# A gated attention and bilinear-FFN mix on one core: gate sums in the K/V projection, Q moved inside SBUF, and the front written as one list of operations

## The chip, the core and the metric

The kernel runs on one core of a Trainium2 chip. Five engines work side by side: TensorE (PE, with the loads of its stationary operand shown as PEld), VectorE (DVE), ScalarE (ACT), GpSimd (POOL), and SyncE (SP), whose queue here issues nearly all transfers. Each engine takes its own instructions strictly in the order in which the kernel wrote them, and waits where one of them needs something that another engine or a transfer has not yet delivered. The metric is the device time of the program in microseconds (us), lower is better. Before the change it is 1620.87 us, the median of three runs (1620.53 to 1621.84).

## The reference

The input `x` is 2048 tokens of 512 numbers. Attention has 32 heads of size 16 that share one K and one V; the other branch is a bilinear FFN with 1792 inner columns; a sigmoid gate per token mixes both.

```python
x = A_x
g = _sigmoid((x * gate_w).sum(-1, keepdims=True))
# a: attention
q = (x @ wq).reshape(B, S, H, Dh).transpose(0, 2, 1, 3)    # H = 32, Dh = 16
k = x @ wk
v = x @ wv
p = _softmax(jnp.einsum("bhqd,bkd->bhqk", q, k) * (Dh ** -0.5), axis=-1)
a = jnp.einsum("bhqk,bkd->bhqd", p, v).transpose(0, 2, 1, 3).reshape(B, S, H * Dh) @ wo
# b: bilinear FFN
b = jnp.einsum("bsf,fd->bsd", (x @ w_gate) * (x @ w_up), w_down)
return g * a + (1 - g) * b
```

All is fp32. The kernel writes a product of two fp32 matrices as three products of a rounded high part and a low remainder (hi·hi, lo·hi, hi·lo), which `mm3` lists.

## The kernel before, in words

**Units.** The attention is cut into 64 units, one for each chunk `c` of 512 tokens, group `g` of 8 heads (128 columns of `wq`) and tile `t` of 128 tokens. For each unit PE computes the scores twice. The first pass (S1, the function `p1`) puts queries on partitions and keys along the row, 512 keys at a time; DVE takes the maximum of each 512 keys (`mx`). Sixteen steps (4 head slots by 4 key chunks `kq`), each with two halves, give 32 maxima for a unit. `p1_end` folds them into one maximum per query and head, DVE splits it into two parts, four small DMAs store it in DRAM (`dm`), and two DMAs fetch it as two extra rows of the unit's `Q` tile. The second pass (S2, `p2`) then computes the scores with keys on partitions and the maximum already taken off, ACT takes the exponential into a `P` tile, and `pv` multiplies `P` with V (`acc`). `osb`, `do`, `raw`, `rb` and `oT` belong to the division and transposition of the result. Two halves of 64 array rows run side by side on PE, called lanes here, and S1, S2 and all the products of the steady part go out on lane 0 or lane 1.

**Filler.** The projections of Q for the other chunks and groups, the FFN and the product with `wo` are cut into jobs of 12 products per lane (`Job`), which are woven between S1, S2 and `pv`. In the first chunk, group 0's Q is projected in the front, and groups 1 to 3 are jobs.

**What sets the order.** The front (from `x_trans0` to the last `kv`) is written out by hand. Then a planner takes over: the class `State` counts with fixed costs and due times, and a loop first gives the lead: S1 until both lanes have `LEAD` = 25 steps, and `LEADJOBS` = 6 jobs of filler. After the lead, tokens of the string `ORDER` say which of S1, filler, S2 or `pv` comes next; the first S2 of unit 0 is held back in the plan until `mat[0]`, the time at which its maximum should have come back. On the chip PE waits there for the fetch itself. `later` and `at` place work of the other engines and queues by the plan's clock.

**The front.** The chunks of `x` are loaded in order (`load_x`), transposed by PE into `px` banks (`x_trans0`, `x_trans`), copied by ACT to a high part and subtracted by DVE or POOL to a low part (`split`). `kv` multiplies with `wkvt`, a 128-column weight that holds K three times (high, low, high rows for the three products of S1) and V, for 512 tokens at once; ACT and DVE write `KK`, ACT a copy for V, which `v_trans` transposes. Q of group 0 is stored to DRAM and fetched by `q_fetch` with six DMAs for each unit, since a unit's `Q` tile has another arrangement of partitions. In the trace below, L296 is the DVE step that finishes `KK`, L700 the maximum, L143 a DVE split, L303 the copy of V.

**Gate.** The sum of `x * gate_w` per token is taken in the lead: POOL multiplies (L320), ACT sums with an accumulator (L324), 16 times; `gates` then makes the sigmoid.

Of the kernel before, what the change touches and what calls it, by code (L numbers as in the profile page):

```python
# [21 lines left out]
D = 512  # L22
# [26 lines left out]
LEADJOBS = 6  # L49
# [6 lines left out]
)  # L56

# [11 lines left out]
def mix_kernel(ctx: ExitStack, tc: tile.TileContext, x, wq, wk, wv, wo, wg, wu, wd, gw, out):  # L69
# [34 lines left out]
    z = consts.tile([128, NC * NT], F32, name="z")  # L104
# [58 lines left out]
    def load_x(c):  # L163
        if c < 2:
            xn = [w512("y", F32, 8) for _ in range(NT)]
        else:
            pairs = [work.tile([128, 2, 512], F32, name="P", tag="P", bufs=PBUF) for _ in range(2)]
            xn = [t[:, i] for t in pairs for i in range(2)]
        for t in range(NT):
            eng = nc.scalar if c == 0 and t == NT - 1 else nc.sync  # L170
            eng.dma_start(xn[t], x2[c * 512 + t * 128:c * 512 + t * 128 + 128, :])
        return xn
# [33 lines left out]
    def q_store(c, g, qh, ql):  # L206
        dq[c, g] = []
        for src in (qh, ql):
            d = dram.tile([128, 512], F32, name="dq", tag="dq", bufs=2 * NC * NG)
            nc.sync.dma_start(d, src.bitcast(F32))  # L210
            dq[c, g].append(d)
        dqat[c, g] = clock["T"] + 4500.0
# [5 lines left out]
    def q_fetch(u):  # L218
        c, g, t = units[u]
        q = Q[u] = work.tile([128, 4, 128], F32R, name="Q", tag="Q", bufs=QB)  # L220
        for d, rows in zip(dq[c, g], ((0, 32), (16,))):
            for half in range(2):
                for r in rows:
                    b = half * 64 + r
                    src = d[half * 64:half * 64 + 64, t * 128:(t + 1) * 128]
                    nc.sync.dma_start(q[b:b + 16].bitcast(F32), src.rearrange("(s d) q -> d s q", d=DH))
        qat[u] = clock["T"] + 6000.0

    kvn = work.tile([128, 4, 32], F32, name="kvn", tag="oT", bufs=2)
    nc.scalar.dma_start(kvn[:, :, 0:16], wk_v)  # L230
    nc.scalar.dma_start(kvn[:, :, 16:32], wv_v)
    xns = {0: load_x(0)}
    wqn = [stage(wq_v[:, :, 0:128])]
    xns[1] = load_x(1)
    xns[2] = load_x(2)
    xns[3] = load_x(3)
    wqs = [[w512("wh", F32R, WB), w512("wl", F32R, WB)] for g in range(NG)]
    kvs2 = [work.tile([128, 4, 32], F32R, name=n, tag=n, bufs=2) for n in ("rb", "raw")]
# [4 lines left out]
    def kv_split():  # L243
# [8 lines left out]
        split2(*wqs[0], wqn[0])  # L252

    def x_trans0():
        xT[0] = x_tiles()
        hi, lo = xT[0][2:]
        for t in range(NT):
            p = bank(2 + t, "px")
            for k in range(4):
                nc.tensor.transpose(p[:, KS[k]], xns[0][t][:, KS[k]], ident)  # L260
            split(hi[:, :, KS[t]], lo[:, :, KS[t]], p.rearrange("p (k q) -> p k q", k=4))
            if t == 1:
                kv_split()

    def x_trans(c, ks=range(4), pool=()):
        xn = xns[c]
        if c not in xT:
            xT[c] = [[w[:, k] for k in range(4)] for w in (woh, wol)] if c == 3 else \
                x_tiles((("hh", "hl"), ("wdh", "wdl"))[c - 1])
        for k in ks:  # L270
            p = bank(2 + (4 * c + k) % 5, "px")
            for t in range(NT):
                nc.tensor.transpose(p[:, KS[t]], xn[t][:, KS[k]], ident)  # L273
            if k in pool:
                xs = w512(("yt", "osb")[k % 2], F32, 2)
                nc.scalar.copy(xT[c][0][k], p)
                nc.scalar.copy(xs, p)
                nc.gpsimd.tensor_tensor(xT[c][1][k], xs, xT[c][0][k].bitcast(F32), op=OP.subtract)
            else:
                split(xT[c][0][k], xT[c][1][k], p)  # L280

    kvs = {}

    def kv(c, between=None):
        p = ms_bank(c % 2)
# [3 lines left out]
        mm_all(p, prods[:6], True, False)  # L289
        if between:  # L290
            between()
        mm_all(p, prods[6:], False, True)
        Kc = KK[:, c * 512:(c + 1) * 512]
        kvs[c] = w512("gs", F32, 3)
        nc.scalar.activation(Kc, p, AF.Identity, bias=kneg)
        nc.vector.scalar_tensor_tensor(Kc, Kc.bitcast(F32), klow, p, op0=OP.mult, op1=OP.add)  # L296
        nc.scalar.copy(kvs[c], p)

    def v_trans(c):
        pv = bank(7, "pv")  # L300
        for t in range(4):
            nc.tensor.transpose(pv[:, t * 128:(t + 1) * 128], kvs[c][:, t * 128:(t + 1) * 128], ident)  # L302
        nc.vector.tensor_copy(V[:, c * 4:(c + 1) * 4, 0:DH].rearrange("p t (h d) -> p t h d", h=2),  # L303
                              pv.rearrange("p (t h c) -> p t h c", t=4, h=2)[:, :, :, 50:58])
# [8 lines left out]
    gate_left = [(c, t) for c in (2, 3, 0, 1) for t in range(NT)]  # L313

    def gate_sum():
        if not gate_left:
            return
        c, t = gate_left.pop(0)
        scr = w512("yt", F32, 2)
        nc.gpsimd.tensor_tensor(scr, xns[c][t], gwb, op=OP.mult)  # L320
        end = spend("pool", 1240.0)

        def add():
            nc.scalar.activation(scr, scr, AF.Copy, accum_out=z[:, c * NT + t:c * NT + t + 1])  # L324
            spend("act", 700.0)
            gate_sum()
# [674 lines left out]
```

## Time and profile before

| | us |
|---|---|
| median of 3 runs | 1620.87 |
| the profiled execution's own time | 1621.27 |
| its span in the profile | 1619.5 |
| PE busy in the span | 1610.8 (99%) |
| DVE busy | 1381.0 (85%) |
| ACT busy | 1245.7 (77%) |
| POOL busy | 744.7 (46%) |
| first S1 on PE | 22.44 |
| last row of the front on PE, first row of the lead | 31.87, 32.19 |
| 32 maxima of unit 0 done, fold begins on DVE | 49.41 |
| first S2 on PE | 58.74 |
| first `acc` product on PE | 70.08 |

A page of the profile describes one execution. A timeline row gives the start, the length, the engine, the line and operation, the tiles, how many of them run on in one stretch (x15), and in brackets the idle time ahead and what ended it. A chain row gives a start, a length and the work that the end of the program hangs on. A matmul's modelled length is longer than the distance to the next one, so the pace of PE is read from starts, or from a count over a stretch. Rows of SPq are the issue of a DMA, not its transfer.

### The profile page before, as it was taken

The page shows a single profiled execution, that of the slowest core. Times are in us where ns is not written, and L with a number is a line of the kernel's source. Part 1 is how long each engine was busy: PE and PEld are TensorE (multiplying, and loading weights), DVE is VectorE, ACT ScalarE, POOL GpSimd, SP SyncE. Part 2 cuts the span into 40 slices and gives each one's busy share as a digit, 9 for nine tenths or more (in the row PEclk, how much of TensorE's full clock was granted, in tenths as well). Part 3 has the DMA queues.
Part 4 walks back from the last instruction along what each step waited for, and adds up shares of the span by engine and source line. Part 5 has one row for each costly group of instructions (what it writes and reads, how often), then busy time and mean ns, then how long its engine had stood idle before and what let it go on. Part 6 is the DMA issues. An engine that isn't in the chain of part 4 may idle for free.

```text
span 1619.5 us, 35319 instructions
## 1 busy us (share of the span) xinstructions
PE 1610.8 (99%) x13126; PEld 1042.4 (64%) x13126; DVE 1381.0 (85%) x2410; ACT 1245.7 (77%) x2411; POOL 744.7 (46%) x876
## 2 busy tenths in 40 slices
PE   9999999999999999999999999999999999999998
PEld 7666666666666666666666666576566666666664
DVE  6988888888898888888888888888888898898870
ACT  4787777777788787787778787787788787787785
POOL 5515652624644642635443651643743641642732
PEclk9999999999999999999999999999999999999999
DMA  4463322212312221212231221222231221222101
GB/s 161 174 212 114 97 67 59 61 54 72 102 58 72 66 73 54 65 52 69 64 100 62 71 66 57 64 59 65 62 111 52 68 79 53 62 65 60 36 25 38
DMA packets 184991, 121.44 MB, mean 75 GB/s; under 512 B 46196, under 2 KB 154356, under 8 KB 184820
## 3 DMA queue, kind: packets, MB, share of 16 engines
q1 hardware_dynamic: 183620, 118.87, 24.5%
q8 instruction: 103, 1.69, 0.4%
q14 instruction: 68, 0.56, 0.1%
q10 hardware_dynamic: 1200, 0.33, 0.1%
HBM read 82.96 MB, written 36.17 MB: 74 GB/s over the span
## 4 chain that ended last, share of the span: by engine, by line
PE 97%; DVE 1%; ACT 1%; issue 0%; POOL 0%; POOLq 0%; ACTq 0%
PE ms L872 34%; PE acc L753 29%; PE s L740 18%; PE s L699 15%; DVE mx L700 1%; PE ms L150 1%; ACT P L741 1%; PE px L273 0%; PE wo L150 0%; PE warm L764 0%; ACT yt L361 0%; PE pv L302 0%; PE pick L672 0%; PE px L260 0%; DVE rb L675 0%
## 5 line engine op out<-in xcount | busy, mean ns | idle before, releaser
L700 DVE TENSOR_REDUCE mx<-s 128x1 f32<-128x512 f32 x2048 | 1306.9, 684 | 171.2 <-PE s L699 87.9
L741 ACT ACTIVATE P<-s 128x512 f32<-128x512 f32 x2048 | 1077.9, 605 | 257.1 <-PE s L740 188.0
L740 PE MATMUL s<-Q,KK 50*128 50x512 f32 x2048 | 750.3, 411 | 0.1
L699 PE MATMUL s<-KK,Q 48*128 48x512 f32 x2048 | 692.7, 407 | 0.1
L753 PE MATMUL acc<-P,V 128*32 128x512 f32 x4096 | 492.9, 598 | 0.0
L740 PEld LDWEIGHTS s<-Q,KK 50*128 50x128 f32 x2048 | 352.6, 185 | 175.6 <-issue 97.2
L699 PEld LDWEIGHTS s<-KK,Q 48*128 48x128 f32 x2048 | 338.6, 185 | 104.0 <-ACT P L741 47.3
L872 PE MATMUL ms<-xh,wh 64*128 64x512 f32 x920 | 338.9, 391 | 0.0
L872 PE MATMUL ms<-xl,wh 64*128 64x512 f32 x920 | 336.5, 391 | 0.0
L872 PE MATMUL ms<-xh,wl 64*128 64x512 f32 x920 | 322.6, 392 | 0.0
L753 PEld LDWEIGHTS acc<-P,V 128*32 128x32 f32 x4096 | 107.9, 109 | 236.2 <-issue 195.4
L535 POOL TENSOR_TENSOR hf<-gs 128x512 f32<-128x512 f32 x56 | 72.0, 1285 | 351.8 <-ACT gs L526 337.0
L362 POOL TENSOR_TENSOR y<-y,yt 128x512 f32<-128x512 f32 x79 | 101.5, 1288 | 233.4 <-ACT yt L361 229.8
L872 PEld LDWEIGHTS ms<-xl,wh 64*128 64x128 f32 x920 | 164.6, 186 | 8.2
L872 PEld LDWEIGHTS ms<-xh,wh 64*128 64x128 f32 x920 | 163.5, 185 | 9.6 <-issue 0.4
L872 PE MATMUL ms<-wdh,hh 64*128 64x512 f32 x448 | 164.6, 393 | 0.0
L872 PE MATMUL ms<-wdl,hh 64*128 64x512 f32 x448 | 164.2, 391 | 0.0
L872 PEld LDWEIGHTS ms<-xh,wl 64*128 64x128 f32 x920 | 157.8, 186 | 9.8 <-issue 0.3
L872 PE MATMUL ms<-wdh,hl 64*128 64x512 f32 x448 | 158.9, 392 | 0.0
L138 POOL TENSOR_TENSOR wl<-wn,wh 128x512 fp32r<-128x512 f32 x116 | 149.5, 1289 | 9.3
L757 ACT COPY osb<-acc 128x512 f32<-128x512 f32 x64 | 37.6, 587 | 75.8 <-PE acc L753 75.8
L635 POOL TENSOR_TENSOR oT<-raw,rb 128x128 f32<-128x128 f32 x63 | 29.1, 463 | 128.3 <-DMA rb<-dr 128.3
(149 smaller groups left out, 1343.4 us busy)
## 6 DMA issues: line engine op xcount, KB each, us to landing
do<-osb SPq DMA_DIRECT2D x63, 256.0 KB
wn<-in_B_w_gate_dram SPq DMA_DIRECT2D x56, 256.0 KB
wn<-in_B_w_up_dram SPq DMA_DIRECT2D x56, 256.0 KB
wdn<-in_B_w_down_dram SPq DMA_DIRECT2D x56, 256.0 KB
Q<-dq SPq DMA_DIRECT2D x384, 32.0 KB
raw<-do SPq DMA_DIRECT2D x252, 32.0 KB
dq<-oh SPq DMA_DIRECT2D x16, 256.0 KB
dq<-ol SPq DMA_DIRECT2D x16, 256.0 KB
```

The lines of the kernel that those rows point to most:

```text
L138: nc.gpsimd.tensor_tensor(lo, src, hi.bitcast(F32), op=OP.subtract)
L150: nc.tensor.matmul(p, l, r, start=start and i == 0, stop=stop and i == len(prods) - 1)
L362: nc.gpsimd.tensor_tensor(y[c, t], y[c, t], tmp, op=OP.add)
L535: nc.gpsimd.tensor_tensor(hf, gu[0], gu[1], op=OP.mult)
L635: nc.gpsimd.tensor_tensor(dst, raw[:, 0], rb, op=OP.mult)
L699: nc.tensor.matmul(p, q[r, slot], KK[r, kq * 512:(kq + 1) * 512], start=True, stop=True)
L700: nc.vector.tensor_reduce(mx[u][:, half * 4 + slot, kq:kq + 1], p, axis=AX.X, op=OP.max)
L740: nc.tensor.matmul(p, KK[r, j * 128:(j + 1) * 128], q[r].rearrange("p s q -> p (s q)"), start=True, stop=True)
L741: nc.scalar.activation(P[s][:, half], p, AF.Exp, scale=0.25)
L753: nc.tensor.matmul(acc[u][b:b + 32, :], V[:, j + i], src[:, half], start=(j == 0), stop=(j == NJ - 2))
L757: nc.scalar.copy(osb, acc.pop(u))
L872: nc.tensor.matmul(p, lhs[HALVES[l]], rhs[HALVES[l]], start=(i == 0 and (l == 0 or j.apart)), stop=(end and (l == 1 or j.apart)))
```

## The change

It has four parts.

1. **Gate sums.** `gate_w` is loaded as 4 rows of 128 (`gwn`), transposed by PE, and becomes a 33rd column of the K/V weight (`kvn`), split with it and placed in column 58 of `wkvt`. The projection `kv` then yields the gate's sum as one of its 128 rows; `v_evac` takes its exponential with ACT, 4 columns for a chunk. The 16 products of POOL, the 16 sums of ACT, the load of `gwb` and the tile `z` are gone.
2. **Q from SBUF to SBUF.** Q of chunk 0, group 0 is projected in two halves of 256 tokens (`q_first` 0 and 4). Units 0 and 1 need the first half; `q_move` carries it from the split tile to `Q` with six DMAs for each unit, no DRAM between. For the other units `q_store` now writes six pieces (high, low, high, two halves each) with six DMAs for a job instead of two, arranged so that `q_fetch` needs two DMAs for a unit instead of six. The columns of `wq` are permuted when split (`wq_split`), which gives this arrangement.
3. **The front as one list.** The string `FRONT` names each operation of the front by a letter and numbers: D, C and L load, T transposes, X and P split (P with POOL), K is a quarter of a `kv` product, E its evacuation, V and U the transposition of V and its evacuation, J a quarter of a Q product, Z its evacuation, M a move, N, A and W weight splits, S one half of an S1 step. Q of group 1 joins the front, so `FRONTQ` = (2, 3) are left as jobs, and `LEADJOBS` is 5.
4. **Order of S1.** `order1` begins with key chunk 0 of unit 0 and of unit 1, then goes on with chunks 1 to 3 of unit 0. Unit 0 has its 32 maxima after 40 half steps instead of 32. The front holds 22 half steps instead of 8; the lead still ends at 25 steps a lane.

Rows of the built program show three places. First PE, from the end of chunk 1's `kv` product to the first S1 rows. `px` are transposes of x, `s` is S1, `pv` the transposition of V. Before:

```order
L150 MATMUL ms_325<-hl,P 128x512
L302 MATMUL pv<-ident,gs 128x128 x4
L273 MATMUL px<-ident,P 128x128 x8
L699 MATMUL s_367<-KK,Q 128x512
L699 MATMUL s_370<-KK,Q 128x512
```

and after, from the transposition of chunk 0's V on:

```order
L318 MATMUL pv<-ident,gs 128x128 x4
L281 MATMUL px<-ident,P 128x128 x4
L157 MATMUL kv<-hh,P 128x512 x2
L157 MATMUL kv<-hl,P 128x512
L157 MATMUL kv<-hh,P 128x512 x2
L157 MATMUL kv<-hl,P 128x512
L729 MATMUL s_335<-KK,Q 128x512
L729 MATMUL s_342<-KK,Q 128x512
L729 MATMUL s_345<-KK,Q 128x512
```

S1 began behind the whole product of chunk 1 (its last row is the first one shown) and 8 transposes of chunk 3. Now its first three halves stand inside chunk 1's product (`kv<-hh`), ahead of all transposes of chunk 3, and the groups of S1 that follow alternate with the rest of the front.

Second SP, from the store of unit 0's maximum (`dm<-mt`) to its fetch (`Q<-dm`) and the next fetch of a unit (`Q<-dq`). `dq` is the store of a Q job. Before:

```order
L720 DMA dm<-mt 8x2x32 x4
L226 DMA Q<-dq 16x4x128 x6
L210 DMA dq<-oh 128x512
L210 DMA dq<-ol 128x512
L727 DMA Q<-dm 2x512 x2
L226 DMA Q<-dq 16x4x128 x6
```

and after:

```order
L750 DMA dm<-mt 8x2x32 x4
L222 DMA dq<-oh 64x512 x2
L222 DMA dq<-ol 64x512 x2
L222 DMA dq<-oh 64x512 x2
L757 DMA Q<-dm 2x512 x2
L234 DMA Q<-dq 48x4x128 x2
```

Eight issues stood between the store and its fetch. Now six stand there, all of one job (chunk 0, group 3); the first of them waits for ACT and the third for POOL to deliver that job.

Third POOL, in the stretch from the end of the front into the lead. Before, the products of the gate (L320) stand among the low parts of Q (L344):

```order
L320 TENSOR_TENSOR yt<-P,osb 128x512 x8
L320 TENSOR_TENSOR yt<-y,osb 128x512
L344 TENSOR_TENSOR ol<-gs,oh 128x512
L320 TENSOR_TENSOR yt<-y,osb 128x512 x2
L344 TENSOR_TENSOR ol<-gs,oh 128x512
L320 TENSOR_TENSOR yt<-y,osb 128x512 x2
L344 TENSOR_TENSOR ol<-gs,oh 128x512
L320 TENSOR_TENSOR yt<-y,osb 128x512 x3
L344 TENSOR_TENSOR ol<-gs,oh 128x512 x7
```

and after they are gone; splits of x (L294, `wdl` and `wol`) stand where POOL now ends the front, then the last split of `wq` (L144, L145) and the low parts of Q (L370):

```order
L294 TENSOR_TENSOR wdl<-yt,wdh 128x512
L294 TENSOR_TENSOR wol<-yt,woh 128x512
L294 TENSOR_TENSOR wol<-osb,woh 128x512
L144 CAST wh<-wn 128x512
L145 TENSOR_TENSOR wl<-wn,wh 128x512
L370 TENSOR_TENSOR ol<-gs,oh 128x512
L370 TENSOR_TENSOR ol<-gs,oh 128x256
L370 TENSOR_TENSOR ol<-gs,oh 128x512 x9
```

POOL has 16 instructions of 512 columns less in the lead, and three splits of x more in the front.

From the first S2 on, PE's rows are the same in both programs, row for row but for line numbers, and so are ACT's but for the gate's exponential (L330), which is no longer there. Ahead of it PE has 50 halves of S1, 64 transposes of x and the same number of products in both, except that 12 products of 512 columns are now 24 of 256, and one transpose of 4 columns is added.

The diff, cut to its core:

```diff
-LEADJOBS = 6
+LEADJOBS = 5
+FRONT = """
+D1 D3 T01 X01 D0 L0 D2 T03 T00 T02 A0 C1 X00 X03 J00 J01 N X02 J02 J03 T10 C2 L1 T12 K00 K01 Z0 T11 M0 X12 K02 K03 P10
...
+FRONTQ = (2, 3)
...
     def q_store(c, g, qh, ql):
-        dq[c, g] = []
-        for src in (qh, ql):
-            d = dram.tile([128, 512], F32, name="dq", tag="dq", bufs=2 * NC * NG)
-            nc.sync.dma_start(d, src.bitcast(F32))
-            dq[c, g].append(d)
+        d = dq[c, g] = dram.tile([2, 3, 64, 512], F32, name="dq", tag="dq", bufs=NC * NG)
+        for r, src in enumerate((qh, ql, qh)):
+            for half in range(2):
+                nc.sync.dma_start(d[half, r], src[HALVES[half]].bitcast(F32))
...
-        for d, rows in zip(dq[c, g], ((0, 32), (16,))):
-            for half in range(2):
-                for r in rows:
-                    b = half * 64 + r
-                    src = d[half * 64:half * 64 + 64, t * 128:(t + 1) * 128]
-                    nc.sync.dma_start(q[b:b + 16].bitcast(F32), src.rearrange("(s d) q -> d s q", d=DH))
+        for half in range(2):
+            src = dq[c, g][half, :, :, t * 128:(t + 1) * 128]
+            nc.sync.dma_start(q[half * 64:half * 64 + 48].bitcast(F32), src.rearrange("r (d s) q -> (r d) s q", s=4))
...
+    gwn = work.tile([128, 128], F32, name="gwn", tag="rb", bufs=2)
+    nc.scalar.dma_start(gwn[0:4], gw.rearrange("(k p) -> k p", p=128))
...
+            eng.tensor_copy(w[:, :, 0, 58:59], kvs2[v][:, :, 32:33])
+    def wq_split(g, fn):
+        n = wqn[g].rearrange("p (m s d) -> p m d s", s=4, d=DH)
+        fn(*[w.rearrange("p (m d s) -> p m d s", d=DH, s=4) for w in wqs[g]], n)
...
+    def v_evac(c):
+        pv = vp.pop(c).rearrange("p (t h c) -> p t h c", t=4, h=2)
+        nc.vector.tensor_copy(V[:, c * 4:(c + 1) * 4, 0:DH].rearrange("p t (h d) -> p t h d", h=2), pv[:, :, :, 50:58])
+        nc.scalar.activation(gb[:, c * NT:(c + 1) * NT], pv[:, :, 0, 58], AF.Exp, scale=-1.0)
...
-        nc.gpsimd.tensor_tensor(scr, xns[c][t], gwb, op=OP.mult)
...
-            nc.scalar.activation(scr, scr, AF.Copy, accum_out=z[:, c * NT + t:c * NT + t + 1])
...
+    def q_first(g, i):
+        if i == 0:
+            qp[g] = hold(("q", g), "q")
+        cols = slice(0, 256) if g == 0 else slice(256, 512) if g == NG else slice(0, 512)
+        prods = [(w, xk[:, cols]) for w, xk in proj(wqs[g % NG], xT[0])]
+        mm_all(qp[g][:, cols], prods[3 * i:3 * i + 3], i == 0, i == 3)
+    def q_move(u):
+        qh, ql = qp["s"]
+        Q[u] = work.tile([128, 4, 128], F32R, name="Q", tag="Q", bufs=QB)
+        for r, src in ((0, qh), (32, qh), (16, ql)):
+            for half in range(2):
+                b = half * 64 + r
+                eng = nc.scalar if u == 0 and half else nc.sync
+                eng.dma_start(Q[u][b:b + 16].bitcast(F32), src[HALVES[half], KS[u]].bitcast(F32))
...
-    order1 = [(0, slot, kq) for kq in range(4) for slot in range(4)]
-    order1 += [(u, slot, kq) for u in range(1, NU) for slot in range(4) for kq in range(4)]
+    order1 = [(u, slot, 0) for u in range(2) for slot in range(4)]
+    order1 += [(u, slot, kq) for u in range(2) for kq in range(1, 4) for slot in range(4)]
+    order1 += [(u, slot, kq) for u in range(2, NU) for slot in range(4) for kq in range(4)]
...
+    nc.tensor.transpose(p[:, 0:4], gwn[0:4], ident[0:4, 0:4])
+    nc.vector.tensor_copy(kvn[:, :, 32], p[:, 0:4])
...
+    for op in FRONT.split():
+        acts[op[0]](*map(int, op[1:]))
```

More of the change, by code (lines that the diff above doesn't have):

```diff
@@ L251, in kv_split @@
             eng.tensor_copy(w[:, :, :, 50:58], kvs2[v][:, :, 16:32].rearrange("p k (h d) -> p k h d", h=2))
[L252 to L263, printed above, removed]
@@ L265, in x_trans @@
-    def x_trans(c, ks=range(4), pool=()):
-        xn = xns[c]
-        if c not in xT:
[L268 to L280, printed above, removed]
@@ L561, in ffn_jobs @@
         for c in range(NC):
-            yield from q_jobs(c, range(c == 0, NG))
+            yield from q_jobs(c, FRONTQ if c == 0 else range(NG))
         pend = None
```

164 lines of the change are left out of this document (84 added, 80 removed).

## The prediction

> **What bounds the kernel now.** I read the page's engines first, then the chain of waits over the first 75 us, since all that moves stands there, then the timelines of DVE, SP and PE.
>
> ```profile
> PE 1610.8 (99%) x13126; PEld 1042.4 (64%) x13126; DVE 1381.0 (85%) x2410; ACT 1245.7 (77%) x2411; POOL 744.7 (46%) x876
> ```
> ```profile
> 8.82 5.73 PE ms L150 x24
> 14.56 3.86 PE px L273 x32
> ...
> 40.32 9.07 DVE mx L700 x15
> 49.41 0.20 DVE mm L708
> ...
> 50.33 9.57 DVE mx L700 x16
> 59.94 0.50 PE s L699
> ```
>
> PE bounds the whole, but up to 59.94 the chain hangs on DVE's maxima: PE has no free bank until DVE has read one. From 59.94 on the chain is PE's alone. PE's rows are the same in both programs from the first S2 on, so what the change is worth is the shift of that point, and the question is when PE can run S2 at full pace.
>
> ```profile
> 57.90 0.97 PE L699 MATMUL s<-KK,Q 48*128 48x512 f32 x3
> 58.74 0.49 PE L740 MATMUL s<-Q,KK 50*128 50x512 f32 x1
> ```
> ```profile
> 58.74:63.74 5.00, 4.81 (x34) 3.18 (x35) 5.00 (x9) 3.98 (x8) 1.28 (x1) 1.00 0.77 272
> 63.74:68.74 5.00, 5.00 (x43) 3.60 (x41) 4.45 (x8) 4.84 (x10) 1.29 (x1) 1.00 0.17 62
> ```
>
> First S2 starts at 58.74. The second fence counts instructions in stretches of 5 us (PE's in the first bracket): 34, then 43. The 9 that are missing are 9/43 of 5 us, 1.05 us that DVE's backlog costs behind the first S2.
>
> **The change, part by part.** First when S1 can start. Its rate and start before, and the prices of PE's pieces:
>
> ```profile
> 22.98 1.29 DVE L700 TENSOR_REDUCE mx<-s 128x1 f32<-128x512 f32 x2
> ```
> ```profile
> 5.50 0.59 ACT L142 CAST xh<-px 128x512 fp32r<-128x512 f32 x1 [1.88 <-PE px L260]
> 6.12 1.51 DVE L143 TENSOR_TENSOR xl<-px,xh 128x512 fp32r<-128x512 f32 x2 [3.94 <-ACT xh L142]
> 6.24 0.86 PEld L260 LDWEIGHTS px<-ident,y 128*128 128x128 f32 x8 [0.33 <-DMA y<-in_A_x_dram]
> 8.82 2.09 PE L150 MATMUL ms<-xh,P 128*128 128x512 f32 x8 [1.48 <-DVE P L251]
> 14.40 1.91 PE L273 MATMUL px<-ident,y 128*128 128x128 f32 x16
> 25.43 0.40 PE L150 MATMUL ms<-wdl,P 128*128 128x512 f32 x1
> 25.75 0.50 PE L699 MATMUL s<-KK,Q 48*128 48x512 f32 x2
> 26.18 0.74 PE L150 MATMUL ms<-wdh,P 128*128 128x512 f32 x2
> ```
>
> A product of 512 columns comes every 0.23 us (24 of the chain in 5.73, transitions included, 0.24), four transposes take 0.46 (1.91/4, less the last one's length), and a pair of S1 in between costs 26.18 - 25.43 - 0.23 = 0.52, of which 0.29 is the change of array rows. The new list has J0 (Q of 256 tokens) first. It needs the low part of two x tiles; the x tile that comes by the ACT queue lets PE on at 6.24, the tile that J0 needs is transposed right behind it, so its copy starts 1.1 to 1.3 later, at 7.5, and its low part is done at 8.75. From there to the first S1, PE does 10 products of 256, 21 of 512 and nine groups of transposes (eight of x, one of V). A product of 256 is not in the trace: at least a transpose's 0.115, at most the 0.23 of 512 columns. I take 0.13, since half the columns should take half of 0.23 and the load of the stationary operand is paced as in a transpose; at 0.23 all is 1.0 later. Sum: 10 x 0.13 + 21 x 0.232 + 9 x 0.46 = 10.3, so S1 at 19.05 + 0.3 = 19.4 and the first maximum 0.45 later, 19.85. That is 3.1 earlier than 22.98. The move of Q starts when J0's split is done, about 11.3, and has 8 us to land.
>
> Then DVE to the end of unit 0, which now has 40 maxima before it, not 32:
>
> ```profile
> 12.60 0.75 DVE L296 SCALAR_TENSOR_TENSOR KK<-KK,klow,ms 128x512 fp32r<-128x512 f32 x1 [2.73 <-ACT KK L295]
> 15.83 2.47 DVE L143 TENSOR_TENSOR hl<-px,hh 128x512 fp32r<-128x512 f32 x4
> 22.63 0.22 DVE L303 COPY V<-pv 128x64 f32<-128x64 f32 x1
> 40.32 9.06 DVE L700 TENSOR_REDUCE mx<-s 128x1 f32<-128x512 f32 x15 [0.44 <-PE s L699]
> 50.24 18.07 DVE L700 TENSOR_REDUCE mx<-s 128x1 f32<-128x512 f32 x29
> ```
>
> 40 x 0.615 (between 9.06/15 and 18.07/29) + 3 splits x 0.62 + 3 x 0.74 for KK + 3 x 0.2 for V = 29.3. PE's list sends S1 in groups of 2 to 4 with 0.5 to 3.5 us between; laid beside each other, DVE runs dry ahead of the groups behind the transposes of chunk 3 and lightly twice more, 1.5 us in all. So unit 0's maxima end at 19.85 + 29.3 + 1.5 = 50.65, against 49.41: the earlier start is more than spent on eight maxima of unit 1.
>
> Then the way of the maximum through DRAM, which S2 waits for:
>
> ```profile
> 50.10 0.23 DVE L714 TENSOR_REDUCE mt<-mt 128x32 fp32r<-128x64 f32 x1
> ```
> ```profile
> 50.35 1.34 SPq L720 DMA_DIRECT2D dm<-mt  x4
> 51.74 2.64 SPq L226 DMA_DIRECT2D Q<-dq  x6
> 54.48 0.37 SPq L210 DMA_DIRECT2D dq<-oh  x1
> 54.95 0.38 SPq L210 DMA_DIRECT2D dq<-ol  x1
> 55.38 0.75 SPq L727 DMA_DIRECT2D Q<-dm  x2
> ...
> 103.89 0.61 SPq L631 DMA_DIRECT2D rb<-dr  x1
> ```
> ```profile
> 106.43 0.46 POOL L635 TENSOR_TENSOR oT<-raw,rb 128x128 f32<-128x128 f32 x1 [3.18 <-DMA rb<-dr]
> ```
>
> Before, 9.33 us pass from 49.41 to S2: 0.94 on DVE, 1.34 for four issues, 3.7 behind eight other issues, 0.75, then at most 2.6 to land. A small fetch that an engine really waited for landed 106.43 - 104.50 = 1.9 after its issue ended, so 58.74 hung on DVE, not on the fetch (56.13 + 1.9 = 58.03). After, six issues stand between, 6 x 0.37 = 2.2 if their data is there: 50.65 + 0.94 + 1.34 + 2.2 + 0.75 + 1.9 = 57.8. The job they carry ends on PE some 2 us behind the 40th S1, near 51; two ACT copies (0.6 each) and POOL's 1.29 put its low part at 52.4 to 54.0, where the third issue wants it at 53.7. So 57.8 to 58.1; I take 57.9.
>
> PE is there by then: the front from 8.75 on is, with the same prices, 48 products of K/V and 12 of Q (13.9), 22 of 256 left (2.9), 16 groups of transposes (7.4), and eight groups of S1 (4.9), 29.1, so 37.9; the lead has 60 products and 14 S1 on one lane, 74 x 0.232 = 17.2, which gives 55.1. PE then waits 2.8 us for unit 0's maximum.
>
> DVE has only 10 maxima left in that wait (6.2 us from 51.6) and no backlog, so the 1.05 us behind S2 falls away. Sum: 57.9 - 58.74 - 1.05 = -1.9.
>
> What I cost at nothing: the 16 products on POOL and 16 sums on ACT are removed in a lead that hangs on DVE; POOL and ACT are on the chain there nowhere. The extra columns add a few copies of 0.2 us or less to engines that idle in the first 20 us, POOL's extra splits and the strided splits of `wq` end 4 us or more before their product. In the steady part SP issues fewer DMAs; PE's waits there name a transfer once:
>
> ```profile
> PEld s L740 <- DMA xd<-wdh: 0.8, 1, 0.8
> ```
>
> so fewer issues are worth 0.8 at most, and four more stores for a job cost nothing while that stays so.
>
> The profiled execution took 1621.27 (0.4 above the median of 1620.87) with 1.8 around its span of 1619.5. From the median: 1620.87 - 1.9 = 1619.0.
>
> A slow TensorE at the start speaks against the change. The transposes behind the warm-up come 0.21 apart, those from 14.40 on 0.12:
>
> ```profile
> 1.36 3.25 PE L764 MATMUL warm<-ident 128*128 128x128 f32 x14 [1.36 <-POOL ident masks.py:199]
> 4.40 2.94 PE L260 MATMUL px<-ident,y 128*128 128x128 f32 x16
> ```
>
> PE now waits for `gwn`, the third load of its queue, ahead of the transposes. If that gap kept the slow pace through the first tiles and J0, 12 transposes and 10 products would take 0.1 more each: S1, and with it S2, 2.2 later, and the time 1621.2. I give that 4 in 100, as PE already waited at 6.24 and was fast right after. The Trainium skill, TensorE: Matmul & The Clock Gate, Part 1, has the clock halved until some 3.4 us of sustained activity in a window that runs freely; the doubled pace agrees, though the granted clock reads 1.00 in that stretch too.
>
> **The rivals.** *PE's bill decides (faster).* If the list leaves DVE no gap and the fetch's way is as short as its parts (0.94 + 1.34 + 0.75 + 1.9, and 1.1 for the store to land, 6.0), S2 comes at 49.15 + 6.0 = 55.15, PE's own 55.1, and the time is 1620.87 - 3.6 - 1.05 = 1616.2. It counts as faster from S2 at 56.55 on. For it: S1 that starts 3.1 us earlier, and parts that the rows show one by one. Against: eight more maxima, and six issues ahead of the fetch. 40 in 100.
>
> *The store of Q blocks the fetch (slower).* The fetch of the maximum stands on SP behind a store that waits for POOL's low part. Each us that this is late makes S2 a us late: it turns to a loss when the low part comes after 55.7 (S2 at 59.8), and to one above 0.2% after 58.9, 1624.1. It needs a job that is 5 us later than I reckon, for instance by ACT waiting for the earlier job's stores, six now where there were two. 14 in 100, with later landings.
>
> *The forecast* is 42 in 100, with 1617.7 to 1621.0 as its own range.
>
> **How the numbers follow.** A measurement of this kernel can tell about 0.2%, 3.2 us, from no change. Forecast and slow start are within it: 0.46; faster 0.40; slower 0.14. The likeliest is 1619.0. The range goes down to PE's bill less a us for prices that are a little too high, 1615.2, and up to 1623.0, which leaves out most of the slower case.
>
> **What would show it.** First maximum at 19.9 (23 before), unit 0's fold at 50.7, the first S2 at 57.9 with PE idle ahead of it and naming the fetch of `dm`, 43 instructions in the 5 us behind it. A fold before 49 or an S2 before 56.5 makes me wrong towards faster; a fetch issued after 57 towards slower. A steady part that takes another time between the same two instructions would upset the whole argument, which says that nothing changes there.

## The result, and the profile after

The changed kernel takes 1633.61 us, the median of 6 runs (1632.41 to 1635.11), against 1620.72 of the kernel before (6 runs, 1620.44 to 1621.84). The ratio is 1.0079, with a 95% interval of 1.0066 to 1.0092: slower by 12.9 us, where 1.9 us faster had been predicted. The profiled execution has a span of 1632.3 us, 12.8 above the 1619.5 of before.

The page's engines, PE's waits and the chain answer to the views shown of before. First the engines, then the groups of PE's waits (who waited for what: us in total, times, longest):

```profile
PE 1616.7 (99%) x13127; PEld 1050.5 (64%) x13127; DVE 1380.5 (85%) x2410; ACT 1238.4 (76%) x2388; POOL 728.9 (45%) x863
```
```profile
PE s L770 <- DMA Q<-dm: 5.3, 2, 4.2
...
PE warm L795 <- DMA gwn<-in_gate_w_dram: 1.1, 1, 1.1
PE s L770 <- ACT P L771: 0.9, 1, 0.9
...
PE px L281 <- DMA y<-in_A_x_dram: 0.6, 1, 0.6
```

Before, no group of PE's waits named `dm` or an exponential. PE's share still reads 99%, since the share counts matmuls that run at half pace as busy too. From the chain over the first 125 us, two stretches:

```profile
59.76 0.60 SPq L222
60.41 2.42 DMA dq<-oh
63.00 0.63 ACT oh L369
...
114.92 0.59 SPq L222
...
116.68 2.38 DMA Q<-dm
119.11 0.77 PE s L770
```

SP and its transfers are on the chain with three kinds of work: the stores of Q (L222), the landing of a store that still holds the tile `oh` that ACT wants next, and the fetch of unit 2's maximum. Where the time went is seen when the same points of the program are laid beside each other. `u2b` and `warm1` are experiments below, with the same rows on PE.

| us | before | after | `u2b` | `warm1` |
|---|---|---|---|---|
| first maximum on DVE | 22.98 | 22.95 | 21.70 | 20.28 |
| unit 0's fold | 49.41 | 54.09 | 52.86 | 51.41 |
| first S2 | 58.74 | 62.99 | 59.80 | 58.35 |
| first S2 of unit 2 | 109.10 | 119.11 | 110.29 | 108.84 |
| span | 1619.5 | 1632.3 | 1621.2 | 1619.6 |

Of the 12.8 us, 4.25 are there at the first S2 and 10.0 at unit 2. Another 1.6 follow right behind unit 2: the S2 row that starts at 133.59 before starts at 145.16 after, 11.6 later. The windows around it, PE's count in the first bracket and PEclk behind POOL:

```profile
110.00:120.00 10.00, 5.81 (x45) 2.20 (x44) 4.92 (x11) 2.74 (x7) 0.00 (x0) 0.96 0.79 229
120.00:130.00 10.00, 10.00 (x76) 8.21 (x75) 8.11 (x12) 9.04 (x18) 1.75 (x2) 0.87 0.85 217
130.00:140.00 10.00, 10.00 (x86) 6.21 (x84) 8.86 (x18) 8.48 (x17) 6.67 (x8) 1.00 0.51 116
```

From 130 on, PE issues its usual 84 to 88 in 10 us. So 11.6 us are lost in the first 125 us. The other 1.3 come in steps of some tenths over the 1500 us behind them (the last product with `wo` starts at 1628.13, against 1615.24 before), and no run explains them.

### The profile page after: what moved, and what is told of

Same layout as the page of the kernel before. It is cut to its first block, busy times and chain, and to the rows that moved or that the text cites. A ratio compares the mean times of both kernels' runs of the same rounds, so it can differ in the third digit from the quotient of the medians.

```text
span 1632.3 us, 35076 instructions
## 1 busy us (share of the span) xinstructions
PE 1616.7 (99%) x13127; PEld 1050.5 (64%) x13127; DVE 1380.5 (85%) x2410; ACT 1238.4 (76%) x2388; POOL 728.9 (45%) x863
## 4 chain that ended last, share of the span: by engine, by line
PE 96%; SPq 1%; ACT 1%; DMA 1%; issue 0%; POOL 0%; DVE 0%; ACTq 0%; POOLq 0%
PE ms L888 33%; PE acc L783 29%; PE s L770 18%; PE s L729 14%; SPq L222 1%; ACT P L771 1%; PE kv L157 1%; PE px L281 0%; PE q L157 0%; DMA dq<-oh 0%; DMA y<-in_A_x_dram 0%; PE wo L157 0%; DMA Q<-dq 0%; POOL ol L370 0%; ACT oh L369 0%
## 5 line engine op out<-in xcount | busy, mean ns | idle before, releaser
L145 POOL TENSOR_TENSOR wl<-wn,wh 128x512 fp32r<-128x512 f32 x115 | 148.8, 1294 | 9.2
```

Source lines behind the costliest of these rows:

```text
L145: nc.gpsimd.tensor_tensor(lo, src, hi.bitcast(F32), op=OP.subtract)
```

## Experiments: which part of the change costs

Two theories stood against each other. Theory A: the six-piece store of Q holds SP, and with it the small transfers behind it. Theory B: the front itself is late. The first run undoes the store alone, the second makes it alone on the kernel before, the third undoes the order of S1, the fourth moves the gate column.

**`u2b`: the changed kernel with two stores and six fetches.** Only SP's instructions differ.

```
 def q_store(c, g, qh, ql):
-    d = dq[c, g] = dram.tile([2, 3, 64, 512], F32, ...)
-    for r, src in enumerate((qh, ql, qh)):
-        for half in range(2):
-            nc.sync.dma_start(d[half, r], src[HALVES[half]].bitcast(F32))
+    dq[c, g] = []
+    for src in (qh, ql):
+        d = dram.tile([128, 512], F32, ...)
+        nc.sync.dma_start(d, src.bitcast(F32))
+        dq[c, g].append(d)
...
+                nc.sync.dma_start(q[b:b + 16].bitcast(F32), src.rearrange("(d s) q -> d s q", d=DH))
```

> The changed kernel with Q stored by two transfers of 128 rows for a job and fetched by six for a unit, as before the change; all engines' instructions are those of the changed kernel, only SP's differ. Theory A (the six-piece store holds SP, and through SP the fetches of the maxima and the split tiles): PE's wait of 4.2 us at 119.1 and ACT's 4.4 us for the tiles `oh` are gone, the first S2 comes at 60 to 62 instead of 62.99, and the time is 1622 to 1625.5. Theory B (the front itself is late: it reaches the first S1 at 22.48 and unit 0's fold at 54.09, and everything hangs on that): the time stays at 1630 or above.

Measured: 1622.98 us (11 runs, 1622.56 to 1623.88), ratio to before 1.0010 (1.0001 to 1.0019). PE's wait for `dm` and ACT's wait for `oh` are gone and the first S2 comes at 59.80, just ahead of the 60 to 62 expected. Theory A has it: 10.6 of the 12.9 us are the store, by the medians. The profiled spans differ by 11.1: 3.2 at the first S2 (62.99 against 59.80), 5.6 more at unit 2 (119.11 against 110.29 is 8.8), and 2.3 behind that. But 1.25 of the 3.2 is no work of the store: the first maximum already came at 21.70 instead of 22.95, and the first store of Q is issued at 36.2 in `u2b` and at 37.5 in the changed kernel. PE's pace at the start differed between these two executions, as the runs on the front show below.

**`o2b`: the kernel before with the six-piece store, the fetch in two and the permuted `wq` alone.** PE, DVE, ACT and POOL have the order of before.

```
 def q_store(c, g, qh, ql):
-    for src in (qh, ql):
-        d = dram.tile([128, 512], F32, ...)
-        nc.sync.dma_start(d, src.bitcast(F32))
+    d = dq[c, g] = dram.tile([2, 3, 64, 512], F32, ...)
+    for r, src in enumerate((qh, ql, qh)):
+        for half in range(2):
+            nc.sync.dma_start(d[half, r], src[HALVES[half]].bitcast(F32))
...
-        split2(*wqs[g], wqn[g])
+        n = wqn[g].rearrange("p (m s d) -> p m d s", s=4, d=DH)
+        split2(*[w.rearrange("p (m d s) -> p m d s", d=DH, s=4) for w in wqs[g]], n)
```

> The kernel before with this part of the change alone: the six-piece store of Q, the fetch in two pieces and the permuted split of `wq`; PE's, DVE's, ACT's and POOL's order is that of before, only SP's differs. Theory A: the time grows by 6 to 10 us, to 1627 to 1631, with a wait of PE for a fetch of the maximum somewhere between 100 and 130 us and ACT waiting for `oh`. Theory B: within 2 us of before, 1619 to 1623.

Measured: 1635.26 us, 1.0090 (1.0076 to 1.0104), 14.1 us slower than before; more than theory A expected, since here group 0's Q goes through the six pieces too, ahead of the first S1. PE's and ACT's waits:

```profile
PE s L737 <- DMA Q<-dm: 3.2, 2, 1.7
PE s L737 <- ACT P L738: 2.6, 2, 1.7
...
PE s L696 <- DMA Q<-dq: 1.6, 2, 1.1
```

These 7.4 us of waits are half of the 14.1. The granted clock read 0.83, 0.66 and 0.83 in the windows 20:30, 60:70 and 110:120 of this run, so a wait costs more than its length; `delay` measures that below.

**`u4`: the changed kernel with S1 in the order of before**, 32 maxima ahead of unit 0's fold.

```
-order1 = [(u, slot, 0) for u in range(2) for slot in range(4)]
-order1 += [(u, slot, kq) for u in range(2) for kq in range(1, 4) for slot in range(4)]
-order1 += [(u, slot, kq) for u in range(2, NU) for slot in range(4) for kq in range(4)]
+order1 = [(0, slot, kq) for kq in range(4) for slot in range(4)]
+order1 += [(u, slot, kq) for u in range(1, NU) for slot in range(4) for kq in range(4)]
```

> The changed kernel with S1 in the order of before (all of unit 0 first, 32 maxima ahead of its fold), the rest of the change kept. Theory A: the fold comes 8 x 0.61 = 4.9 us earlier, at about 49.2, but the fetch of its maximum still stands behind the stores on SP and the wait at 119 stays; the time is 1630 to 1633. Theory B: the earlier fold carries S2 with it, 4 to 5 us earlier, and the time is 1628 to 1629.5.

Measured: 1635.84 us, 1.0090 (1.0076 to 1.0104), above both expectations. The fold came at 48.4 and the fetch was issued at 54.6, but the first S2 still stood at 63.23: with this order the planner puts two fences (a transpose on PE that waits for a copy on DVE) into the program, one on either side of the first S2, and PE waits 2.6 us for them, with a granted clock of 0.83 in 60:70. The wait at unit 2 is 4.4 us here too. An earlier fold brought no earlier S2 here, but the fence stands in the way; `u24` repeats it without the store.

**`gfix`: the gate column out of the way of the first transposes.** The load of `gwn` goes behind x tile 3 on ACT's queue; its transpose and copy move to just ahead of the weight split N.

```
-nc.scalar.dma_start(gwn[0:4], gw.rearrange("(k p) -> k p", p=128))
...
-D1 D3 T01 X01 D0 ... J00 J01 N X02 ...
+D1 D3 H T01 X01 D0 ... J00 G J01 N X02 ...
...
+def g_load():
+    nc.scalar.dma_start(gwn[0:4], gw.rearrange("(k p) -> k p", p=128))
+def g_col():
+    p = hold("g", "warm")
+    nc.tensor.transpose(p[:, 0:4], gwn[0:4], ident[0:4, 0:4])
+    nc.vector.tensor_copy(kvn[:, :, 32], p[:, 0:4])
+    release("g")
```

> The changed kernel with the load of `gwn` behind that of x tile 3 on ACT's queue, and its transpose on PE and copy on DVE just ahead of the weight split instead of ahead of the first transposes of x. Both theories: the first transposes start at 4.4 to 4.8 instead of 5.9, and x tile 3 lets PE on 0.7 us earlier. Theory A: unit 0's fold comes about 1 us earlier, the time falls by 0.5 to 1.5 us, to 1632 to 1633, since the stores set the end. Theory B: the whole gain in the front goes through, 1.3 us or more, to below 1632.4.

Measured: 1639.83 us, 1.0112 (1.0096 to 1.0127), 6.2 slower than the changed kernel, against both theories. The transposes did start at 4.40, but PE then stayed at half pace longer (the first maximum at 24.3, against 22.95), and the bank that `g_col` takes and returns gives all later operations another bank. PE's timeline of this run:

```profile
45.04 0.49 PE L894 MATMUL ms<-xh,wh 64*128 64x512 f32 x1 [1.87 <-ACT gb L322]
...
47.21 0.62 PE L894 MATMUL ms<-xl,wh 64*128 64x512 f32 x1
47.64 0.62 PE L894 MATMUL ms<-xh,wh 64*128 64x512 f32 x1
...
57.20 0.50 PE L894 MATMUL ms<-xh,wh 64*128 64x512 f32 x1
```

The first job's bank was one that the gate's exponential still read, so PE waited 1.87 us. Two microseconds later every product of a lane comes 0.43 us behind the last one instead of 0.23, for 10 us, and the granted clock reads 0.50 from 48 to 56. The fold came at 61.1. So this run doesn't price the place of `gwn`.

## Experiments: what a wait of PE costs

**`delay`: `u2b` with 14 added stores ahead of unit 2's fetch of its maximum.** It puts the wait at 119 back into a kernel that has none.

```
 def fetch():
+    for i in range(14 if u == 2 else 0):
+        nc.sync.dma_start(dram.tile([128, 128], F32, name="dump", ...), ident)
```

> The kernel `u2b` with 14 added stores of 64 KB (`ident` to DRAM) ahead of unit 2's fetch of its maximum on SP, nothing else: 14 x 0.35 = 4.9 us, of which some 1.7 are slack, so PE waits 3 to 3.5 us near 110. If a wait costs its length and no more: 1626 to 1626.6. If PE's pace halves behind it, as it did behind the wait at 119.1 in the changed kernel, 1 to 2.5 us more: 1627 to 1629. If later work takes the wait up: below 1625.

Measured: 1629.85 us, 1.0052 (1.0039 to 1.0064), 6.9 above `u2b`; a little over the case of a halved pace, as the wait too came out longer than reckoned.

```profile
114.86 0.79 PE L776 MATMUL s<-Q,KK 50*128 50x512 f32 x1 [4.41 <-DMA Q<-dm]
...
115.87 0.63 PE L894 MATMUL ms<-woh,wl 64*128 64x512 f32 x1
...
116.30 0.63 PE L894 MATMUL ms<-wol,wh 64*128 64x512 f32 x1
...
120.07 0.39 PE L894 MATMUL ms<-woh,wh 64*128 64x512 f32 x1
...
120.30 0.39 PE L776 MATMUL s<-Q,KK 50*128 50x512 f32 x1
```

One wait of 4.41 us is followed by 5.2 us (114.86 to 120.07) in which a lane's products come 0.43 apart instead of 0.23. That loses about 5.2 x (1 - 0.23/0.43) = 2.4, and 4.4 + 2.4 = 6.8 is the 6.9 measured.

**`delay9`: the same with 9 stores.**

```
-    for i in range(14 if u == 2 else 0):
+    for i in range(9 if u == 2 else 0):
```

> The kernel `delay` with 9 added stores instead of 14. Those 14 took 8.2 us of SP (0.585 each) and made PE wait 4.41, so 3.8 was slack; 9 take 5.3, so PE waits 1.4 to 1.6 us. If half pace follows only a longer wait: 1624.3 to 1624.9. If it follows this one too, for some 5 us as in `delay`: 1626.3 to 1627.5.

Measured: 1626.44 us, 1.0033 (1.0020 to 1.0045), 3.5 above `u2b` for a wait of 2.04 us.

```profile
113.57 0.50 PE L776 MATMUL s<-Q,KK 50*128 50x512 f32 x1 [2.04 <-DMA Q<-dm]
...
115.46 0.62 PE L894 MATMUL ms<-woh,wh 64*128 64x512 f32 x1
...
115.89 0.62 PE L776 MATMUL s<-Q,KK 50*128 50x512 f32 x1
...
118.72 0.39 PE L776 MATMUL s<-Q,KK 50*128 50x512 f32 x1
...
118.95 0.39 PE L894 MATMUL ms<-wol,wh 64*128 64x512 f32 x1
```

PE runs at full pace for 1.5 us behind the wait, and at half pace from 115.08 to 118.45, 3.4 us, which costs 1.6, so the sum is 3.6 where 3.5 was measured. (The profiled execution's span is 4.8 above that of `u2b`; the 1.2 more stand there at the first S2 already, 60.97 against 59.80.) A wait of 2 us was enough here, and the half pace began when the wait was over. The Trainium skill, TensorE: Matmul & The Clock Gate, Part 1, describes this: the clock is halved or released by windows of some 3.4 us that run freely. The length of 3.4 us agrees; that a window must be idle as a whole, as the page has it for the fall, does not, since any window of 3.4 us that holds this wait also holds 1.4 us of matmuls. Not every wait is followed by half pace: behind the changed kernel's wait of 1.09 us at 62.99 the granted clock stayed at 1.00.

## Experiments: why the store holds SP

Prices of SP's issues, from the groups by line, of `u2b` (whole stores of 128 rows, 256 KB) and of the changed kernel (64 rows, 128 KB); the three numbers are minimum, median and maximum in ns:

```profile
L222 SPq DMA_DIRECT2D dq<-oh x16: 319/360/1490, 36.2 to 141.4; - x16
L222 SPq DMA_DIRECT2D dq<-ol x16: 320/375/411, 37.6 to 142.8; - x16
```
```profile
L222 SPq DMA_DIRECT2D dq<-oh x64: 446/595/1292, 37.5 to 160.1; - x64
L222 SPq DMA_DIRECT2D dq<-ol x32: 445/594/1477, 38.8 to 158.8; - x32
```

Half the bytes are issued in 1.6 times the time: 6 x 0.595 = 3.6 us a job, against 2 x 0.37 = 0.7. Three runs ask whether this is the issue or the bytes, of which the six pieces write half as many again.

**`s3b`: `u2b` with the high part stored a second time, whole.** The bytes of the changed kernel, with three issues.

```
-    for src in (qh, ql):
+    for src in (qh, ql, qh):
...
-        for d, rows in zip(dq[c, g], ((0, 32), (16,))):
+        for d, rows in zip(dq[c, g], ((0,), (16,), (32,))):
```

> The kernel `u2b` with the high part of Q stored a second time, whole, for its own row of the fetch: three stores of 128 rows for a job, each into a tensor of its own, six fetches for a unit as in `u2b`. The bytes stored are those of the changed kernel, 768 KB for a job, but SP issues only one store more. Theory A (SP's issue time is what costs): one more issue of 0.4 to 0.5 us for a job, 1623 to 1625. Rival A2 (the bytes, and the tile `oh` held until its second store has landed): 1628 or above, with ACT waiting for `oh`.

**`s4`: `u2b` with each of its two stores cut into two of 64 rows.** The bytes of `u2b`, four issues.

```
-        nc.sync.dma_start(d, src.bitcast(F32))
+        for half in range(2):
+            nc.sync.dma_start(d[HALVES[half]], src[HALVES[half]].bitcast(F32))
```

> The kernel `u2b` with each of the two stores of a job cut into two of 64 rows: the same bytes to the same places as `u2b`, four issues for two, six fetches for a unit. Theory A: 4 x 0.6 = 2.4 us of SP for a job instead of 1.0, so the fetches of the maxima come 1.5 to 3 us later in the first 160 us; of the 10.6 us that the six stores cost, 1 to 5 come back: 1624 to 1628. Rival A2 (bytes): 1622.3 to 1623.7, as `u2b`.

Measured: `s3b` 1624.10 us, 1.0020 (1.0011 to 1.0029), 1.1 above `u2b`, without a wait of PE or ACT for a store. `s4` 1630.08 us, 1.0056 (1.0044 to 1.0069), 7.1 above `u2b`, more than expected, with one wait of PE:

```profile
PE s L775 <- DMA Q<-dm: 4.6, 1, 4.6
```

Half as many bytes again cost 1.1; two issues more, and smaller, with the bytes and the six fetches of `u2b`, cost 7.1. It is SP's time, and theory A stands. `s4` shows the lever: nearly all of its loss is one wait of 4.6 at unit 2, with a granted clock of 0.69 in 110:120, which a few us more of SP turn from slack into a wait.

**`s3`: the six stores joined in pairs,** the same layout in DRAM as the change.

```
-        for half in range(2):
-            nc.sync.dma_start(d[half, r], src[HALVES[half]].bitcast(F32))
+        nc.sync.dma_start(d[:, r], src.bitcast(F32))
```

> The changed kernel, but with each of a Q job's six stores of 64 rows joined in pairs: three stores of 128 rows, the same bytes in the same places, and the fetch in two pieces as changed. Theory A (SP's time per transfer is what costs; a store of 128 rows was issued in 0.35 to 0.39 us, one of 64 rows in 0.60): a job takes 1.1 to 1.2 us of SP instead of 3.6, PE's wait at 119 and ACT's waits for `oh` go, and the time is 1621 to 1624, as with two stores. Rival A2 (the bytes cost: half as many again as before the change, and the tiles `oh` held until they have landed): 1628 or above.

Measured: 1803.63 us, 1.1120 (1.1105 to 1.1135), far outside both. The median issue of `dq<-oh` took 2.3 us and the longest 7.2, and ACT waited 122.2 us for `oh`. The transfer's outermost dimension in DRAM is 2 here (2 x 64 rows). The Trainium skill, DMA: Bandwidth & Descriptors, section "Why a DMA increments its semaphore by 16 and not by 1", says that a transfer is spread over as many engines, up to 16, as divide the outermost dimension of both sides; that would be 2 engines here and 16 for 64 or 128 rows. The stall agrees with it, but no view of this run shows the engines one by one. As a test of issue against bytes the run failed.

**`pq`: the six stores issued by POOL,** behind the low part, SP being freed of them.

```
-            nc.sync.dma_start(d[half, r], src[HALVES[half]].bitcast(F32))
+            nc.gpsimd.dma_start(d[half, r], src[HALVES[half]].bitcast(F32))
```

> The changed kernel with the six stores of a Q job issued by POOL behind the low part instead of by SP: the same transfers and bytes, in another queue. Theory A (what costs is that SP's other transfers stand behind the stores): PE's wait at 119 goes and the time is 1621 to 1625. Rival A2 (bytes and held tiles): 1628 or above, with ACT still waiting for `oh`. If POOL's own issues take long, its low parts come late and PE waits for POOL instead, also above 1628 but with another name in the waits.

Measured: 1629.38 us (1625.09 to 1629.87), 1.0043 (1.0029 to 1.0057): 4.2 better than the changed kernel, yet short of theory A's range. PE's wait for `dm` is gone, and another has come, the one that rival A2 expected:

```profile
65.80 0.62 ACT L369 CAST oh<-gs 128x512 fp32r<-128x512 f32 x1 [3.60 <-DMA dq<-ol]
```
```profile
66.97 0.56 PE L729 MATMUL s<-KK,Q 48*128 48x512 f32 x1 [3.51 <-ACT P L771]
```

ACT's copy to `oh` stands ahead of the exponentials in its queue and waits until the earlier job's stores have landed, and PE waits for the exponentials. With `s3b` the bytes are ruled out as the main cost; the held tiles are not. POOL's issues take 0.52 us each, so the six still need 3.1 us. A job that is stored in six pieces has this second cost in whichever queue: the two buffers of `oh` and `ol` are held longer.

## Experiments: the front

**`warm1`: `u2b` with x tile 3 and `gwn` first on ACT's queue,** ahead of the K and V weights.

```
-nc.scalar.dma_start(kvn[:, :, 0:16], wk_v)
-nc.scalar.dma_start(kvn[:, :, 16:32], wv_v)
+load_first(3)
 nc.scalar.dma_start(gwn[0:4], gw.rearrange("(k p) -> k p", p=128))
+nc.scalar.dma_start(kvn[:, :, 0:16], wk_v)
+nc.scalar.dma_start(kvn[:, :, 16:32], wv_v)
...
-D1 D3 T01 X01 D0 ...
+D1 T01 X01 D0 ...
```

> The kernel `u2b` (two stores and six fetches, the rest of the change kept) with ACT's queue in another order: x tile 3 and `gwn` first, then the K and V weights. Theory (the front of the changed kernel is late because PE waits twice in its first 8 us and runs at half pace behind that): PE does not wait for `gwn`, is let on by x tile 3 at least 1 us earlier than 7.40, the products of 256 columns come every 0.12 us from the first or nearly, the first maximum comes at 20.0 to 20.6 instead of 21.70, the first S2 as much earlier, at 58.1 to 58.7, and the time is 1621 to 1622.2. Rival (the slow pace has another cause, or the gain is taken up by a wait further on): first S2 at 59.5 or later, 1623 or above.

Measured: 1621.31 us (11 runs, 1620.80 to 1622.28), 1.0000 (0.9991 to 1.0009): 1.7 less than `u2b`, as its theory had it, and the kernel before is reached, not beaten. The start of PE's timeline, first of the changed kernel, then of `warm1`:

```profile
5.71 0.26 PE L795 MATMUL warm<-ident,gwn 4*128 4x4 f32 x1 [1.10 <-DMA gwn<-in_gate_w_dram]
...
7.62 2.82 PE L281 MATMUL px<-ident,y 128*128 128x128 f32 x12 [0.60 <-DMA y<-in_A_x_dram]
...
12.86 0.41 PE L157 MATMUL q<-xh,wl 128*128 128x256 f32 x1
13.07 0.41 PE L157 MATMUL q<-xl,wh 128*128 128x256 f32 x1
```
```profile
4.88 3.11 PE L286 MATMUL px<-ident,y 128*128 128x128 f32 x16
...
10.36 0.28 PE L157 MATMUL q<-xh,wl 128*128 128x256 f32 x1
10.48 0.28 PE L157 MATMUL q<-xl,wh 128*128 128x256 f32 x1
```

In the changed kernel PE waits twice, and its products of 256 columns come 0.21 us apart, down to the last one at 13.07. In `warm1` it waits for no load, and they come 0.12 apart. The first maximum is 2.67 earlier than in the changed kernel, at 20.28. Against `u2b`, from which `warm1` differs by this order alone, it is 1.42 earlier, and the first S2 1.45.

How much a wait at the start costs differs from execution to execution. With the same rows on PE up to there, the first maximum came at 20.78 in `u4`, 21.70 in `u2b`, 22.37 in `s3b` and 22.95 in the changed kernel. In `u4` PE waited 0.60 for `gwn` and 1.31 for the x tile and stayed at full pace, 12 transposes in 1.53 us. In `u2b` it waited 0.74 and 1.28; its first four transposes were at full pace (0.66 us for the four), but then the granted clock reads 0.50 from 8 to 11 us. What decides between the two was not tried, and a part of the changed kernel's late start is the luck of its profiled execution. The gain of `warm1` is more than that: the times of its 11 runs all lie below those of the 11 of `u2b`.

**`u24`: `u2b` with the order of S1 of before** (the edit of `u4` on `u2b`).

> The kernel `u2b` with S1 in the order of before: 32 maxima ahead of unit 0's fold, not 40. The planner then puts a fence of two small transposes and copies into the lead, as it did in `u4`. If the fold and its way through DRAM set the first S2, as the prediction had it, the fold at 48.0 to 48.6 brings S2 to 57 or before, and the time to 1619.5 to 1621. If DVE's 50 maxima of the lead set it, whatever their order, S2 stays at 59.5 to 60.5 (later by the fence's wait), and the time is 1622.5 to 1626.

Measured: 1627.20 us, 1.0037 (1.0025 to 1.0050), 4.2 above `u2b`. Unit 0's fold came 3.2 us earlier than in `u2b`, at 49.7, and the first S2 3.2 later, at 62.99. The planner's fences cost PE 2.6 us here again, 1.76 of them ahead of the first S2, so the run doesn't price the order by itself. But without these 1.76 S2 would stand at 61.2, still behind `u2b`. That speaks for DVE's maxima, whose last of the lead ended at 60.76 here, and against the fold.

## Why the prediction was wrong

**"Four more stores for a job cost nothing while that stays so" is the step that failed,** under "what I cost at nothing", and with it the bound of 0.8. It reasoned from waits that the kernel before did not have. A wait that is absent says that there is slack, not how much. Between unit 2's store of its maximum and the fetch, `u2b` issues:

```profile
101.13 1.33 SPq L754 DMA_DIRECT2D dm<-mt  x4
...
102.94 0.38 SPq L222 DMA_DIRECT2D dq<-oh  x1
103.42 0.39 SPq L222 DMA_DIRECT2D dq<-ol  x1
103.85 1.05 SPq L334 DMA_DIRECT2D xd<-wol  x2
105.02 1.17 SPq L761 DMA_DIRECT2D Q<-dm  x2
```

and the changed kernel:

```profile
109.09 1.35 SPq L750 DMA_DIRECT2D dm<-mt  x4
...
110.92 1.14 SPq L222 DMA_DIRECT2D dq<-oh  x2
112.16 2.08 SPq L222 DMA_DIRECT2D dq<-ol  x2
114.28 1.23 SPq L222 DMA_DIRECT2D dq<-oh  x2
115.56 1.08 SPq L330 DMA_DIRECT2D xd<-wol  x2
116.68 0.63 SPq L757 DMA_DIRECT2D Q<-dm  x2
```

From the end of the store (109.09 + 1.35) to the fetch 6.2 us pass instead of 2.6, and the store of the maximum was already late behind other jobs: 8.0 us behind `u2b`, where PE's own rows were 4.6 behind (the last S2 of unit 1, 112.10 against 107.55). The prediction followed SP's queue to the first S2 and not to the units behind it. There PE then waited 4.19 us for the fetch, and the half pace behind the wait (granted clock 0.50 from 120 to 122) took some 1.6 more, of which the prediction had nothing.

**The way of the maximum through DRAM was mis-sized for the same reason.** The sum charged the six issues at 0.37, the price of a store of 128 rows, when the new ones have 64; they took 57.33 to 61.00, 3.7 instead of 2.2. From fold to S2 8.9 us passed, not 7.25, and the fetch was issued from 61.10, past the 57 that the prediction named as its sign of slower. POOL's low part, which the sum set against 53.7, was no cause: SP came to that job's first store only at 57.33, the four stores of the maximum having gone out from 55.71.

**The slower rival named the mechanism** (a store of Q ahead of the fetch on SP, ACT waiting for an earlier job's stores), but asked for a late low part and looked at the first unit alone. It needed neither: SP's own time suffices. Its 1624.1 covers only what is lost by the first S2; the rest is the wait at unit 2 and the half pace behind it.

**The start of S1 and unit 0's fold were off by 3.1 and 3.4 us** (22.95 for 19.85, 54.09 for 50.65). The slow start, which had 4 in 100, is what happened: transposes 0.235 apart, products of 256 columns 0.21 apart up to 13.3 us. The price of 0.13 for such a product holds at full pace (0.12 in `warm1`), where the first maximum came at 20.28, against 19.85 predicted, and the fold at 51.41, against 50.65. So these two terms hold within 0.8 where PE does not wait for a load in its first 8 us; leaving the wait for `gwn` and the later x tile (it let PE on at 7.62, where the sum took over the 6.24 of before) out of the sum was the error. Its size is in part luck: `u2b` and the changed kernel have the same rows on PE, yet came to full pace for good at about 11.2 and 13.3, and `u4`, with waits of 0.60 and 1.31, had it from its first transposes on.

**That the fetch sets the first S2 held in the changed kernel, but not where the stores are out of the way.** In the changed kernel PE idled ahead of S2 and the wait names `dm`, as the prediction had it, for 1.09 us and not 2.8; DVE's last ten maxima of the lead had ended at 60.98:

```profile
62.99 0.46 PE L770 MATMUL s<-Q,KK 50*128 50x512 f32 x1 [1.09 <-DMA Q<-dm]
```

In `warm1` the first S2 stands at 58.35, 0.45 from the 57.9 predicted, but not because of the fetch, which was issued from 55.04: DVE's last ten maxima of the lead end only at 58.30 (52.24 and 6.06 long). PE has no wait there that names `dm`, and its own bill of 55.1 was never reached, since it runs on banks that DVE frees. That the number came close is luck: the prediction has this end of DVE too, 6.2 us from 51.6, which is 57.8, beside the 57.8 of the fetch, and made it no bound. The faster rival fails by the same account: from its fold at 49.15 the last ten maxima would end at 56.3, past its S2 at 55.15.

**The 1.05 us of DVE's backlog fell away in the changed kernel, where little came of it, and not in `warm1`.** In the 5 us behind the first S2 PE issues 43 instructions in the changed kernel, as predicted, and 37 in `warm1`, against 34 before. First the changed kernel, then `warm1`:

```profile
62.99:67.99 5.00, 5.00 (x43) 4.78 (x45) 4.26 (x7) 4.99 (x10) 1.29 (x1) 1.00 0.63 152
```
```profile
58.35:63.35 5.00, 4.79 (x37) 3.48 (x36) 3.01 (x5) 4.05 (x9) 1.29 (x1) 1.00 0.42 143
```

In the changed kernel PE then waits 0.76 at 71.16 for an exponential that stands behind ACT's wait for `oh`, so of 4.25 us it has won back 0.15 by its 100th row. In `warm1` DVE has idle time too, and what holds PE there was not tried. With 0.4 gained at the first S2, `warm1` ends 0.1 later than before; the 0.5 in between lies spread over the program and is not explained.

**"Nothing changes there", said of the steady part, was nearly right** for PE from 130 us on, but for the 1.3 us that no run explains; the prediction took that part to begin at 59.94, some 70 us too early.

## What to carry to other kernels

Before splitting one transfer into several, count the issues on the queue that also carries the small transfers an engine waits for, at the price of the new shape, and find the slack of each such fetch by the time from its landing to its use; that no wait is shown only says the slack is above zero. On the engine that bounds the kernel a wait of 2 us cost 3.5, because half pace followed it; so fill the gaps of its first microseconds, and spend slack elsewhere.

## What was not expected of the hardware

A store of 64 rows and 128 KB takes SP longer to issue (median 0.595 us) than one of 128 rows and 256 KB (0.36 to 0.375), and longer than one of 128 rows and 64 KB (0.43, the added stores of `delay`); why was not tried. PE's pace halved for 3.4 us after a single wait of 2.04 us, and in `gfix` for 10 us after one of 1.87, but not after one of 1.09 in the changed kernel. The same 256 KB as 2 x 64 rows on the DRAM side made the whole kernel 11% slower.
